# Two steps of a decode attention moved in TensorE's order: the turn of o with wo's matmuls, and the turn of q's second half

## The chip, the cores and the metric

The kernel runs on one core of one Trainium2 chip. Its time is the time on the device in microseconds of one execution. Before the change the median of 11 executions is 185.9 us (185.17 to 189.07).

Engines are named as in the profile: PE is TensorE (PEld its loading of weights), DVE VectorE, ACT ScalarE, POOL GpSimd, and SP SyncE, which issues the transfers.

## The reference

Two layers, each an attention with cached keys and values and a gated MLP, for one new token of each of four sequences. Both layers use the same weights and caches.

```python
# B=4, Sq=1, D=512, Hq=32, Hkv=8, Sk=8192, Dh=128, F=1792, W=2048, all bf16
def A(x):                                   # attention
    q = (x @ wq) as (B, 32, 1, 128)
    k, v = the last W=2048 positions of the caches, each kv head for 4 heads of q
    p = softmax(q k^T / sqrt(128))
    return (p v) as (B, 1, 4096) @ wo
def M(x):                                   # gated MLP
    return (sigmoid(x @ w_gate) * (x @ w_up)) @ w_down
x = x + A(layernorm(x)); x = x + M(layernorm(x))
x = x + A(layernorm(x)); x = x + M(layernorm(x))
```

## The kernel before

The whole program is a list of operations. Each `P.op` names an engine, what it reads and writes, the PSUM banks that it uses, and a function that emits the instructions. An operation depends on the last writers of what it reads, on the readers of what it writes, and, for a bank, on all operations of another engine that used the bank before. `_schedule` then puts the operations of each engine in an order by estimated durations, and `_assign_sync` turns the dependencies into semaphore waits. Each engine works through its own order. From the second layer's q on, `P.chain` is set: every TensorE operation then depends on the one written before it, so that TensorE's order is the order in which the program is written.

The transfers go to slots of one large tile in SBUF, `arena`. A slot is taken from a pool and given back when its last reader has been written down (`done`), so SP's order of issues follows from the order of the readers. The keys are loaded once and kept for both layers; all but a few tiles of V are loaded twice.

The second attention (`attn_second`) runs over eight units u = 0 to 7, one for each KV head h = 7 - u, all four sequences together. The first seven (`NW`) go through the wide path:

- `qx(u)`, in `q_unit`: four matmuls (L721) spread a head's q over a block layout, and ScalarE copies it to SBUF (L726).
- `score(u)`, in `softmax_unit`: four matmuls of a mask (L751) and 16 of K (L758) into one PSUM bank.
- `soft(u)`: the maximum on VectorE (L767, L771, L775, L779), the exponential on ScalarE (L782), which also gives the row sums.
- `turn(u)`, in `turn_p`: a permutation matmul (L795, called pp below), a copy on ScalarE (L797) and a 32 by 32 transpose on VectorE (L802). P is kept in one buffer, `prow`: the exponential of u+1 can start only when L802 of u has read it.
- `sum_up(u)`, in `sums`: POOL multiplies the row sums with a mask (L898), TensorE adds over partitions (L903), VectorE takes the reciprocal (L905), POOL spreads it (L908). The sum goes to bank `CB` for unit 0 and to bank `WB` for the others.
- `pv_wide(u)`: 16 matmuls of P with V (L925), VectorE's transpose of the bank (L933), the diagonal (L938), a move between partitions (L940), then on POOL an addition (L942) and the product with the reciprocals (L945).
- `o_back(u)`: two small matmuls (L959, called tr) that turn o to rows of wo in bank `WB` (bank `CB` for unit 6), and a copy on ScalarE (L965). It is written down as a function in `late` and called from the loop.
- `wo(u)`, in `wo_wide`: four matmuls with wo (L978).

The last unit takes another path (`pv_unit`, L844, L862, L1024), with the turn of unit 6 between its two V tiles. Then follow the second MLP's matmuls (L1170), and w_down's (L1210) in three pieces, each with a transfer of its own, and the output.

The second layer's q is made in two halves: the first (units 0 to 3) in `q_second`, the second (units 4 to 7) at the beginning of `attn_second`; `q_turn` transposes such a half on VectorE (L687) and scales it (L691).

The loop of the units in the kernel before:

```python
            for u in range(NW):
                if u == NW - 1:
                    wo(u - 1)
                op[u] = pv_wide(tag(u), hs[u], u % 2, v_tiles[(2, hs[u])])
                turn(u + 1)
                score(u + 2)
                soft(u + 2)
                ...
                sum_up(u + 1)
                qx(u + 3)
                if 0 < u < NW - 1:
                    wo(u - 1)
                if u < NW - 1:
                    op[u] = late.pop(("tr", tag(u)))()
```

Of the kernel before, what the change touches and what calls it, by code (L numbers as in the profile page):

```python
# [278 lines left out]
def build(nc, A_x, A_k, A_v, A_wq, A_wo, B_wg, B_wu, B_wd, out, cfg=None):  # L279
# [8 lines left out]
    NW = cfg.get("NW", 7)  # L288
# [33 lines left out]
    with es:  # L322
# [47 lines left out]
        P = _Plan()  # L370
# [4 lines left out]
        OBS = (4, 5)  # L375
# [13 lines left out]
        def c_dve(n, rate=None):  # L389
            return tm["dve_fix"] + n * (tm["dve_f32"] if rate is None else rate)  # L390
# [36 lines left out]
        def need(name):  # L427
            while name not in where:
                take_load()
            return where[name]  # L430
# [53 lines left out]
        def wq_part(k, c, i):  # L484

            if k == 0:
                return ("wq", c, k), i * SLOT
            return ("wq", (i, c // 2), k), (c % 2) * SLOT
# [33 lines left out]
        def load_v(h, bp, k, n_use):  # L522
# [7 lines left out]
             r=[("ones_f",)], w=[("e", 0)])  # L530
# [6 lines left out]
        for jh in range(2):  # L537
            for bp in range(2):
                for i in range(2):
# [7 lines left out]
                         r=[("ones_f",), ("perm",)], w=[("perm", jh, bp, i)])  # L547
# [5 lines left out]
             r=[("ones_f",)], w=[("msk_s",)])  # L553
        P.op("vector", "msk_s2", 100.0, lambda v: v.tensor_scalar(msk_s[:, :], msk_s[:, :], -1.0e30, None, ALU.mult),
             r=[("msk_s",)], w=[("msk_s",)])
        P.op("gpsimd", "msk_m", 200.0,
             lambda g: g.affine_select(msk_m[:, :], ones_f[:, 0:2], [[-1, 2]], ALU.is_equal, 0.0, base=0, channel_multiplier=1),
             r=[("ones_f",)], w=[("msk_m",)])
        P.op("vector", "sel_f", 200.0,
             lambda v: v.tensor_reduce(sel_f[:, :], perm[:, :].rearrange("p (g x) -> p x g", x=NR), AXX, ALU.add),  # L560
             r=perms, w=[("sel_f",)])
        P.op("gpsimd", "sel_b", 200.0, lambda g: g.tensor_copy(sel_b[:, :], sel_f[:, :]),
             r=[("sel_f",)], w=[("sel_b",)])
        P.op("vector", "sel_r", 100.0,
             lambda v: v.tensor_reduce(sel_r[:, :], sel_f[:, :].rearrange("p (g y) -> p y g", g=2), AXX, ALU.add),
             r=[("sel_f",)], w=[("sel_r",)])
        P.op("vector", "eyew", 200.0,
             lambda v: v.tensor_reduce(eyew[:, 96:128], ident.rearrange("p (a j) -> p j a", a=4), AXX, ALU.max),
             r=[("e", 0), ("eyew0",)], w=[("eyew",)])
        P.op("vector", "maskp", 200.0,  # L570
             lambda v: v.tensor_reduce(maskp[:, :], ident.rearrange("p (a j) -> p a j", a=4), AXX, ALU.max),
             r=[("e", 0)], w=[("maskp",)])
        P.op("vector", "maskb", 100.0,
             lambda v: v.tensor_reduce(maskb[:, :], maskp[:, :].rearrange("p (j b) -> p b j", j=2), AXX, ALU.max),
             r=[("maskp",)], w=[("maskb",)])
# [3 lines left out]
             r=[("eyew",)], w=[("maske",)])  # L579
        P.op("vector", "mod4", 100.0,  # L580
             lambda v: v.tensor_reduce(mod4[:, :], ey.rearrange("p (e m) -> p m e", m=REP), AXX, ALU.max),
             r=[("eyew",)], w=[("mod4",)])
# [4 lines left out]
             r=[("mod4",), ("maskp",)], w=[("selm",)])  # L587
# [4 lines left out]
             r=[("e", 0)], w=[("permo",)])  # L592
# [4 lines left out]
             r=[("sel_r",)], w=[("maskr",)])  # L597

        o = P.op("scalar", "x_in", 1300.0, lambda e: e.dma_start(x_nat, x_d), w=[("prow",)])
# [80 lines left out]
                if not (keep_last and c == NC - 1):  # L680
                    done(name)

        def q_turn(k, i, qb, buf=None, toks=(("e", 0), ("e", 1))):
            buf = ebuf[:, :] if buf is None else buf
            toks = list(toks)
            P.op("vector", "qt%d_%d" % (k, i), c_dve(512),
                 lambda v: v.transpose(buf, ps[:, qb, :].rearrange("p (x k t) -> p x t k", k=32, t=2)),  # L687
                 r=[("qrow", i)], w=toks, banks=(qb,))
            qi = qh[:, i * 64:(i + 1) * 64]
            return P.op("vector", "qc%d_%d" % (k, i), c_dve(64),  # L690
                        lambda v: v.tensor_tensor(  # L691
                            qi.rearrange("p (c b r) -> p c b r", c=4, b=NB),
                            buf.rearrange("p (r c y) -> p c y r", c=4, y=32)[:, :, 0:NB],
                            lnr[:, 0:NB].unsqueeze(1).unsqueeze(3).broadcast_to([128, 4, NB, REP]), ALU.mult),
                        r=toks + [("lnr", 0)], w=[("qh", i)])
# [42 lines left out]
        late = {}  # L738
# [135 lines left out]
        rest = {}  # L874
# [38 lines left out]
        def pv_wide(tag, h, k2, tiles):  # L913
            ob = OBS[k2]
            ew = ebuf[:, k2 * 256:(k2 + 1) * 256].bitcast(BF16).rearrange("p (g n x t) -> p g n t x", g=4, n=2, t=2)
            ss = dict((bp, need(name)) for bp, name in tiles)

            def e_pv(pe):
                last = None
                for n in range(4):  # L920
                    mq, t = n // 2, n % 2
                    for g in range(4):
                        jh, bp = g // 2, g % 2
                        src = tile_ap(ss[bp])[:, (jh * 16 + 8 * mq) * 128:(jh * 16 + 8 * mq + 8) * 128]
                        last = pe.matmul(ps[32 * g:32 * g + 32, ob, :], ew[:, g, mq, t],  # L925
                                         src.rearrange("p (m t d) -> p t m d", t=2, d=128)[:, t], start=(n == 0), stop=(n == 3))
                return last
            P.op("tensor", "PV" + tag, 16 * tm["pe_row"], e_pv,
                 r=tok(ss[0]) + tok(ss[1]) + [("e", k2)], w=[("pso", k2, 0), ("pso", k2, 1)], banks=(ob,))
            for bp, name in tiles:  # L930
                done(name)
            tv, o32, osh, rm, av = (rest[n, k2] for n in ("tv", "o32", "osh", "rm", "A"))
            P.op("vector", "tv" + tag, c_dve(512), lambda v: v.transpose(tv, ps[:, ob, :]),  # L933
                 r=[("pso", k2, 0), ("pso", k2, 1)], w=[("tv", k2)], banks=(ob,), after=(rest["op"],))

            def e_rd(v):
                dg = rest["dg", k2].rearrange("p (m y) -> p m y", m=4)[:, :, 0:128].rearrange("p m (q z) -> p q z m", z=32)[:, :, 0:8, :]
                return v.tensor_reduce(o32.rearrange("p (q x) -> p q x", x=8), dg, AXX, ALU.add)  # L938
            P.op("vector", "rd" + tag, c_dve(128), e_rd, r=[("tv", k2)], w=[("o32", k2)])
            P.op("vector", "sh" + tag, tm["dve_small"], lambda v: v.tensor_copy(osh[0:64, :], o32[64:128, :]),  # L940
                 r=[("o32", k2)], w=[("osh", k2)])
            P.op("gpsimd", "ad" + tag, 250.0, lambda v: v.tensor_tensor(o32[0:64, :], o32[0:64, :], osh[0:64, :], ALU.add),  # L942
                 r=[("o32", k2), ("osh", k2)], w=[("o32", k2)])
            P.op("gpsimd", "av" + tag, 500.0,
                 lambda v: v.tensor_tensor(  # L945
                     av[0:64, :].rearrange("p (x q e) -> p x q e", x=8, q=4),
                     o32[0:64, :].rearrange("p (q x) -> p x q", x=8).unsqueeze(3).broadcast_to([64, 8, 4, 8]),
                     rm[0:64, :].rearrange("p (x e) -> p x e", e=8).unsqueeze(2).broadcast_to([64, 8, 4, 8]), ALU.mult),
                 r=[("o32", k2), ("rm", k2)], w=[("av", k2)])
            late["tr", tag] = lambda: o_back(tag, k2, av)  # L950
# [101 lines left out]
        def attn_second():  # L1052
            hs = list(range(HKV))[::-1]

            def tag(u):
                return "2.%d" % u

            def turn(u):
                turn_p(2, tag(u), u % 2, PBS[0], u < NW)

            def qx(u):
                if u < HKV:
                    q_unit(tag(u), hs[u], u % 2)

            def score(u):
                if u >= HKV:
                    return
                softmax_unit(tag(u), hs[u], True, False)
                for bp in range(2):
                    pool.release(4 * hs[u] + 2 * bp)  # L1070
                fill()

            def soft(u):
                if u < HKV:
                    late.pop(tag(u))()

            def sum_up(u):
                if u < NW:
                    sums(tag(u), u % 2)
                elif u < HKV:  # L1080
                    sums_old(tag(u), u % 2)

            qx(0)
            q_mms(1, 0, OBS[1], (0, 1))
            qx(1)
            score(0)
            score(1)
            qx(2)
            soft(0)
            turn(0)  # L1090
            s = need(wq_part(1, NC - 1, 0)[0])
            left[wq_part(1, NC - 1, 0)[0]] += 1
            q_mms(1, 0, OBS[1], (2, 3))
            wide_buffers(s, P.ops[-1])
            sum_up(0)
            q_turn(1, 0, OBS[1], rest["tv", 1], [("tv", 1)])
            soft(1)
            op = {}

            def wo(u):  # L1100
                wo_wide(tag(u), hs[u], op[u], u % 2, u == 0, u == NW - 2)

            for u in range(NW):
                if u == NW - 1:
                    wo(u - 1)
                op[u] = pv_wide(tag(u), hs[u], u % 2, v_tiles[(2, hs[u])])
                turn(u + 1)
                score(u + 2)
                soft(u + 2)
                if u == NW - 1:  # L1110
                    wo_back()
                sum_up(u + 1)
                qx(u + 3)
                if 0 < u < NW - 1:
                    wo(u - 1)
                if u < NW - 1:
                    op[u] = late.pop(("tr", tag(u)))()
            u = NW

            def between():  # L1120
                wo_compact(tag(u - 1), hs[u - 1], late.pop(("tr", tag(u - 1)))(), (u - 1) % 2)
            wo_unit(tag(u), hs[u], pv_unit(tag(u), hs[u], u % 2, v_tiles[(2, hs[u])], between), u % 2, False, True)
# [143 lines left out]
        v_tiles = {}  # L1266
# [93 lines left out]
```

## Time and profile before

| | us |
|---|---|
| median of 11 runs | 185.9 |
| their range | 185.17 to 189.07 |
| profiled execution, its own time | 189.55 |
| span of that execution, first to last instruction | 187.8 |
| PE busy | 103.7 (55%) |
| DVE busy | 102.2 (54%) |
| ACT busy | 32.9 (18%) |
| POOL busy | 21.4 (11%) |
| transfers on SP's queue | 71.84 MB, 93.8% of the 16 DMA engines' span |
| L733, VectorE's transposes of K (first layer only) | 37.0, 32 of 1202 ns |
| L758, scores | 26.3, 256 of 548 ns |
| L925, P times V of the second attention | 9.6, 112 of 465 ns |
| L959 for DVE's L905, waited | 7.7 in 6 waits |

Matmuls that follow each other overlap, so a mean of 548 ns is not the time that one of them adds. Times of single pieces, such as 153.46, are microseconds from the start of the span. The profile's second part cuts the span in 40 slices of 4.7 us; each digit is a share in tenths. The chain that ended last is followed back from the last instruction, at each step to what released it.

### The profile page before, as it was taken

Reading aid. Unit: us, or ns where it says so; the run is one execution under the profiler, and the core shown is the slowest. Engines: PE = TensorE matmul, PEld = TensorE weight load, DVE = VectorE, ACT = ScalarE, POOL = GpSimd, SP = SyncE. Lnnn points to the kernel's source line nnn. Section 1 sums busy time; section 2 is a strip of 40 time slices with the busy share of each in tenths; the row PEclk is TensorE's granted clock in tenths of the full one; section 3 lists DMA queues with packets and bytes.
Section 4 is the critical chain, followed back from the end, with each engine's and each line's share of the span. In section 5 each row is a group of like instructions: output and inputs, shape, how many; then the busy total and the mean of one; then the engine's idle time right before and its main releaser. Section 6 shows DMA issues by size and latency. Waiting matters only on the chain.

```text
span 187.8 us, 3838 instructions
## 1 busy us (share of the span) xinstructions
PE 103.7 (55%) x1628; PEld 55.3 (29%) x1639; DVE 102.2 (54%) x253; ACT 32.9 (18%) x87; POOL 21.4 (11%) x86
## 2 busy tenths in 40 slices
PE   1434434754707436064367474358596767759692
PEld 1012121342403315033157422213222333326531
DVE  5209997467683554935645441226744666664243
ACT  2002032030212103011020010001323333332011
POOL 6000011010100101001010000000131333333000
PEclk9999999999999999999999999999955999995558
DMA  5999999999999999999999999999999999999700
GB/s 193 420 434 424 422 415 417 417 422 415 415 424 426 420 420 411 421 422 413 417 420 413 401 414 408 331 349 427 375 415 429 424 420 417 415 404 419 290 3 4
DMA packets 12305, 72.09 MB, mean 384 GB/s; under 512 B 1144, under 2 KB 1152, under 8 KB 5632
## 3 DMA queue, kind: packets, MB, share of 16 engines
q1 hardware_dynamic: 12280, 71.84, 93.8%
q8 instruction: 13, 0.21, 0.5%
q10 hardware_dynamic: 8, 0.00, 0.0%
q14 instruction: 4, 0.03, 0.0%
HBM read 71.83 MB, written 0.00 MB: 382 GB/s over the span
## 4 chain that ended last, share of the span: by engine, by line
PE 33%; DMA 27%; DVE 27%; issue 4%; SPq 4%; ACT 3%; DVEq 0%; ACTq 0%
DMA arena<-in_A_v_cache_dram 19%; DVE arena L733 11%; PE ps L758 9%; DMA arena<-in_A_wq_dram 6%; PE ps L844 5%; PE ps L925 5%; SPq L398 4%; DVE nmax L767 3%; DMA arena<-in_B_w_down_dram 3%; PE ps L751 3%; PE ps L1170 2%; DVE ebuf L802 2%; PE ps L1024 2%; DVE nmax L771 2%; ACT prow L782 2%
## 5 line engine op out<-in xcount | busy, mean ns | idle before, releaser
L733 DVE STREAM_TRANSPOSE arena<-arena 128x1024 f32<-128x1024 f32 x32 | 37.0, 1202 | 0.0
L758 PE MATMUL ps<-arena,qbd 128*32 128x512 bf16 x256 | 26.3, 548 | 0.0
L844 PE MATMUL ps<-ebuf,arena 128*128 128x8 bf16 x576 | 17.8, 168 | 9.0 <-DMA arena<-in_A_v_cache_dram 5.4
L751 PE MATMUL ps<-msk_m,msk_s 128*32 128x512 bf16 x64 | 9.0, 555 | 23.0 <-DVE arena L733 21.9
L767 DVE TENSOR_REDUCE nmax<-ps 128x1 f32<-128x512 f32 x16 | 10.9, 681 | 17.4 <-PE ps L758 17.2
L844 PEld LDWEIGHTS ps<-ebuf,arena 128*128 128x128 bf16 x576 | 16.8, 104 | 11.0 <-DMA arena<-in_A_v_cache_dram 6.5
L782 ACT ACTIVATE prow<-ps,nmax 128x512 bf16<-128x512 f32 x16 | 11.0, 688 | 35.2 <-DVE nmax L779 31.6
L726 ACT CAST qbd<-ps 128x256 bf16<-128x256 f32 x16 | 6.0, 372 | 51.7 <-PE ps L758 34.9
L674 PE MATMUL ps<-arena,xn 128*4 128x512 bf16 x64 | 7.9, 578 | 10.3 <-DMA arena<-in_A_wq_dram 7.9
L758 PEld LDWEIGHTS ps<-arena,qbd 128*32 128x32 bf16 x256 | 8.8, 126 | 11.0 <-issue 9.3
L797 ACT CAST prow<-ps 128x512 bf16<-128x512 f32 x16 | 9.4, 586 | 15.3 <-PE ps L795 5.3
L933 DVE STREAM_TRANSPOSE arena<-ps 128x512 f32<-128x512 f32 x7 | 5.0, 717 | 12.2 <-PE ps L925 12.2
L811 POOL CAST s<-psm 128x1 bf16<-128x1 f32 x9 | 1.7, 188 | 84.7 <-ACT prow L782 84.2
L925 PE MATMUL ps<-arena,ebuf 128*32 128x512 bf16 x112 | 9.6, 465 | 0.1
L751 PEld LDWEIGHTS ps<-msk_m,msk_s 128*32 128x32 bf16 x64 | 1.8, 102 | 24.8 <-DVE arena L733 19.0
L687 DVE STREAM_TRANSPOSE ebuf<-ps 128x512 f32<-128x512 f32 x3 | 2.2, 717 | 12.7 <-PE ps L674 12.6
L1170 PE MATMUL ps<-arena,xn 128*4 128x448 bf16 x64 | 7.0, 564 | 2.4 <-DMA arena<-in_B_w_up_dram 1.7
L655 ACT ACTIVATE lnv<-ps 128x4 f32<-128x4 f32 x4 | 0.7, 174 | 42.5 <-PE ps L651 42.5
L802 DVE STREAM_TRANSPOSE ebuf<-prow 128x256 f32<-128x256 f32 x16 | 7.0, 436 | 2.1 <-ACT prow L797 1.9
L721 PE MATMUL ps<-qh,eyew 32*128 32x64 bf16 x64 | 5.7, 220 | 4.1 <-ACT qbd L726 2.4
L852 DVE TENSOR_TENSOR onb<-ps,rinv 128x16 bf16<-128x16 f32 x9 | 1.7, 185 | 10.7 <-PE ps L844 10.7
L1024 PE MATMUL ps<-onp,arena 128*128 128x16 bf16 x144 | 5.3, 175 | 2.4 <-DVE onp L867 2.4
(105 smaller groups left out, 125.4 us busy)
## 6 DMA issues: line engine op xcount, KB each, us to landing
arena<-in_A_v_cache_dram SPq DMA_DIRECT2D x30, 1024.0 KB, 16.3
arena<-in_A_k_cache_dram SPq DMA_DIRECT2D x16, 1024.0 KB, 25.2
arena<-in_A_wq_dram SPq DMA_DIRECT2D x8, 1024.0 KB, 9.6
arena<-in_A_wo_dram SPq DMA_DIRECT2D x4, 1024.0 KB, 24.7
arena<-in_B_w_gate_dram SPq DMA_DIRECT2D x4, 896.0 KB, 14.1
arena<-in_B_w_up_dram SPq DMA_DIRECT2D x4, 896.0 KB, 15.9
arena<-in_B_w_down_dram SPq DMA_DIRECT2D x2, 1024.0 KB, 12.9
arena<-in_B_w_down_dram SPq DMA_DIRECT2D x1, 768.0 KB, 7.4
```

Of the source, the lines that this page charges most:

```text
L674: last = pe.matmul(ps[32 * hh:32 * hh + NB, qb, :], xn[:, c * NB:(c + 1) * NB], tile_ap(s)[:, o + hh * 512:o + (hh + 1) * 512], start=(c = ...
L733: P.op("vector", "T%d_%d" % (h, t), c_dve(1024), lambda v, v32=v32: v.transpose(v32, v32), r=[("slot", 4 * h + t)], w=[("slot", 4 * h + t)])
L751: last = pe.matmul(ps[32 * gi:32 * gi + 32, bank, :], msk_s[:, :], msk_m[:, :].unsqueeze(1).broadcast_to([128, 256, 2]), start=True, stop= ...
L758: last = pe.matmul(ps[32 * gi:32 * gi + 32, bank, :], qbd[:, q0:q0 + 32], kt[:, cp // 2, cp % 2, jh * NJ:(jh + 1) * NJ, :], start=False, s ...
L767: lambda v: v.tensor_reduce(nmax[:, k2:k2 + 1], ps[:, bank, :], AXX, ALU.max),
L782: lambda a: a.activation(prow[:, :].rearrange("p (m x t) -> p m x t", x=32, t=2), ps[:, bank, :].rearrange("p (m t x) -> p m x t", x=32, t ...
L797: P.op("scalar", "pc" + tag, c_act(512), lambda a: a.copy(prow[:, :], ps[:, pb, :]), r=[("ppb", pb)], w=[("prow",)], banks=(pb,))
L802: P.op("vector", "pt" + tag, c_dve(256), lambda v: v.transpose(et, prow[:, :].bitcast(F32)), r=[("prow",)], w=[("e", k2)])
L844: last = pe.matmul(ps[:, ob, bp * 8:bp * 8 + 8], src[:, j * 128:(j + 1) * 128], ev[:, j % 2, j % 16 // 2, x0:x0 + 8], start=(j == 0), stop ...
L925: last = pe.matmul(ps[32 * g:32 * g + 32, ob, :], ew[:, g, mq, t], src.rearrange("p (m t d) -> p t m d", t=2, d=128)[:, t], start=(n == 0) ...
L1024: last = pe.matmul(ps[:, WB, c * NR:(c + 1) * NR], tile_ap(s)[:, o + r_ * D + c * 128:o + r_ * D + (c + 1) * 128], ov[:, r_ * NR:(r_ + 1) ...
L1170: last = pe.matmul(ps[32 * g:32 * g + NB, OBS[n], 0:NF], xn[:, c * NB:(c + 1) * NB], tile_ap(s)[:, o:o + NF], start=(c == 0), stop=(c == N ...
```

## The change

Two things are moved; no instruction is added or taken away.

In the loop, `o_back` of a unit (L959 on TensorE, L965 on ScalarE) is no longer called at the end of that unit's turn of the loop. It is called in the next turn, behind P times V of the next unit and the permutation of the P after it. In TensorE's order `tr` of unit u-1 then stands behind L925 of u and L795 of u+1 and ahead of the scores of u+2. The matmuls with wo of unit u-1 stand at the end of turn u, as before. For the last wide unit the turn of unit 5 is called directly ahead of its wo, where it stood before too.

In the prologue, qx(2) is written behind the exponential and the permutation of unit 0, and the transpose of q's second half is given a dependency on unit 0's L802, so that on VectorE it stands behind it.

On ScalarE the copy L965 then stands behind L797, no longer ahead of it, and the copy L726 of qx(2) stands behind the first L782 and L797. On VectorE L802 of unit 0 and L687 change places. The orders of POOL and SP are the same as before.

```diff
-        def q_turn(k, i, qb, buf=None, toks=(("e", 0), ("e", 1))):
+        def q_turn(k, i, qb, buf=None, toks=(("e", 0), ("e", 1)), after=()):
...
-                 r=[("qrow", i)], w=toks, banks=(qb,))
+                 r=[("qrow", i)], w=toks, banks=(qb,), after=after)
...
             score(0)
             score(1)
-            qx(2)
             soft(0)
             turn(0)
+            qx(2)
...
-            q_turn(1, 0, OBS[1], rest["tv", 1], [("tv", 1)])
+            q_turn(1, 0, OBS[1], rest["tv", 1], [("tv", 1)], [o for o in P.ops if o.name == "pt2.0"])
...
+            def back(u):
+                op[u] = late.pop(("tr", tag(u)))()
+
             for u in range(NW):
                 if u == NW - 1:
+                    back(u - 1)
                     wo(u - 1)
-                op[u] = pv_wide(tag(u), hs[u], u % 2, v_tiles[(2, hs[u])])
+                pv_wide(tag(u), hs[u], u % 2, v_tiles[(2, hs[u])])
                 turn(u + 1)
+                if 0 < u < NW - 1:
+                    back(u - 1)
                 score(u + 2)
                 soft(u + 2)
...
                 if 0 < u < NW - 1:
                     wo(u - 1)
-                if u < NW - 1:
-                    op[u] = late.pop(("tr", tag(u)))()
             u = NW
```

## The prediction

> **What bounds the kernel now.** I read the chain that ended last first. Up to 127.3 us it goes through the transfers; from the third quarter of wq (landing at 127.3) to the end it holds no transfer at all. So the second attention and the second MLP, some 60 us, are bound by engines. Below, u is a unit (one KV head) of the second attention. The chain within one unit at full clock, TensorE's and VectorE's pieces:
>
> ```profile
> 153.10 0.09 DVE arena L905
> 153.33 0.19 PE ps L959 x2
> 153.52 1.01 PE ps L925 x16
> 154.55 0.73 DVE arena L933
> 155.30 0.45 DVE arena L938
> 155.99 0.45 DVE ebuf L802
> 156.43 0.59 DVE nmax L767
> 157.69 0.21 DVE nmax L779
> 157.90 0.09 DVE arena L905
> 158.13 0.19 PE ps L959 x2
> 158.32 0.32 PE ps L925
> ```
>
> It is a closed loop of 4.80 us (153.52 to 158.32): P times V (L925), VectorE's transpose of it, the diagonal, the transpose of P (L802), the whole maximum of the next scores (L767 to L779), the reciprocal (L905), then the turn `tr` (L959), and only then the next P times V. The wait behind it:
>
> ```profile
> PE ps L959 <- DVE arena L905: 7.7, 6, 1.5
> ```
>
> `tr` of unit u writes bank WB, from which VectorE's reciprocal of unit u+1 reads, and that stands last in VectorE's order. P times V of u+1, whose own operand L802 wrote 1.8 us earlier, stands behind `tr`.
>
> Then the clock, by the stretches, whose columns are time, PE, PEld, DVE, ACT, POOL busy, granted clock, DMA share, GB/s:
>
> ```profile
> 136.00:140.70 4.70, 4.68 (x38) 1.22 (x39) 2.01 (x6) 1.36 (x3) 1.51 (x4) 0.50 1.01 418
> 140.70:145.50 4.80, 3.10 (x34) 1.32 (x37) 2.35 (x8) 1.54 (x5) 0.60 (x2) 0.50 1.01 423
> 155.10:159.90 4.80, 3.51 (x57) 1.49 (x49) 3.20 (x11) 1.80 (x6) 1.51 (x4) 1.00 1.01 415
> ```
>
> The first two units ran at half clock: P times V starts at 136.02, 142.70, 148.66, then every 4.80. That is 148.66 - 136.02 - 2 x 4.80 = 3.04 us more than at full clock. (The 9s before 131 are not borne out: L758's 16 matmuls take 1.71 to 1.74 us there, as at half clock.) Last, the transfers:
>
> ```profile
> DMA  5999999999999999999999999999999999999700
> GB/s 193 420 434 424 422 415 417 417 422 415 415 424 426 420 420 411 421 422 413 417 420 413 401 414 408 331 349 427 375 415 429 424 420 417 415 404 419 290 3 4
> ```
> ```profile
> arena<-in_B_w_down_dram SPq DMA_DIRECT2D x1, 256.0 KB, 15.9
> ```
>
> The last piece of w_down (256 KB) is issued at 163.5 and lands 15.9 us later, at 179.4, though its matmuls (L1210, 184.18 to 185.13) come at some 185.0. The engines are thus 5.6 us behind the last transfer in this execution; the stream has been full since its start and does not get shorter by this change.
>
> **What the Trainium skill says.** "TensorE: Matmul & The Clock Gate", in "What overlaps and what doesn't", has matmuls start and end strictly in program order; the trace agrees: L925 waits behind L959. The same page, "What's actually happening", says the array runs at half clock until it has been busy for a window of about 3.4 us and falls back after an idle one; here the scores' 20 matmuls take 2.32 us (138.38 to 140.70) at 0.50 and 1.34 (154.76 to 156.10) at 1.00. "DMA: Bandwidth & Descriptors", "Specifications", gives a fabric ceiling of 435 GB/s; the slices above show 415 to 430, so the stream has no reserve.
>
> **Part 1, the turn behind P times V.** No instruction is added or removed. TensorE's order of a unit was PV(u), pp(u+1), scores(u+2), sum, qx, WO(u-1), tr(u); it becomes PV(u), pp(u+1), tr(u-1), scores(u+2), sum, qx, WO(u-1). On ScalarE the copy behind `tr` moves behind the copy of P (L797). PV(u+1) now waits only for its P and its V.
> What closes the loop next: pp(u+1) needs the exponential of u+1, which needs its maximum, which needs its scores, which stand behind pp(u) in TensorE's order. Its sum at full clock: L767 to L779 1.55 (156.35 to 157.90), to the exponential 0.04 (157.94), from there to pp 0.83 (133.11 to 133.94), pp to scores 0.32 (154.44 to 154.76), two matmuls of `tr` now between them 0.13 (153.33 to 153.46), scores 1.34, to the maximum 0.06 (140.70 to 140.76): 4.27 us. That it isn't less is checked on the engines. VectorE's own list, L933 to L905, is 3.44 (154.55 to 157.99). TensorE needs 0.32 + 0.13 + 2.09 (scores to WO's end, 154.76 to 156.85) + 1.05 = 3.59; PV(u) then ends about as the reciprocal does and VectorE goes on without a gap. The added `tr` in front of the scores waits for POOL's product (L945), which ends 0.67 + 0.25 + 0.2 us after L940, about 2.8 us ahead of its new place, so at nothing; without that cover it would go into the loop one to one. ScalarE's moved copy of 0.17 delays only the copy of qx (L726), needed a unit later. POOL's and SP's lists stay as they are, and SP waits for scores and P times V, which come earlier. The unit falls by 4.80 - 4.27 = 0.53; between pp(2) and pp(6) there are four such.
>
> **Part 2, the prologue.** qx(2) moves behind pp(0). Its copy (L726, 132.84 + 0.37) stood before the first exponential on ScalarE: that starts at 132.53, after L779's end at 132.49, not at 133.11, 0.58 earlier. pp(0) 133.36; qx(2) 0.28 and the last eight matmuls of q's second half follow and end at 134.55 instead of 134.86. POOL's mask and product (0.24 + 0.32, with their gaps 0.63) and the sum give sum(0) at 135.23 and PV(0) at 135.57, against 136.02. The second half of q's turn (L687, 0.72) falls behind the first L802, which then ends at 134.87 instead of 135.96; so the second exponential starts at 134.91, not 136.00. q's second half is wanted only for unit 4, some 10 us later: nothing. Then pp(1) 136.62, the scores end at 138.28, L802 at 138.50, the maximum runs 138.45 to 140.00, pp(2) stands at 140.87. Four units of 4.27: pp(6) at 157.95, the last maximum at 159.80, in the profiled execution 166.16, and at full clock 166.16 - 3.04 - 0.22 (PV at 163.04 took 1.27, not 1.05) = 162.90. So 3.1 us less at equal clock, 6.4 less than this execution. From there on (tr(5), WO(5), PV(6), the tail) the order is unchanged.
>
> **The sum.** Engines: 187.8 - 6.4 = 181.4 us of span. Transfers: 179.4, the last eight matmuls of L1210 0.2, then from L1210's end to the span's end 2.7 (185.13 to 187.83): 182.3. The transfers end last. On the way the V tiles nearly hold: a tile of 1024 KB takes 2.49 us at 421 GB/s, so counted back from 179.4 over the MLP's 5.25 MB (13.1 us) and the tiles of units 6 and 7 (10.0) V of unit 5 is whole at 156.3, wanted at 156.2; V of unit 6 at 161.3, wanted at 162.7. Outside the span the profiled execution has 189.55 - 187.8 = 1.75, so 182.3 + 1.75 = 184.05. This execution is 3.65 above the median of 185.9; at full clock mid-kernel it would be 187.8 - 3.26 + 1.75 = 186.3, near that median, so I take the transfers' end over as it stands: 184.0 us, 1.0% less.
>
> **Rivals.**
> A: the stream ends earlier in other executions. The slices of 331, 349 and 375 GB/s cost, against 418, 0.98 + 0.78 + 0.48 = 2.2 us. Without them the floor is 181.8 and the engines set the end: 185.9 - 3.1 = 182.8, less up to 0.6 for an earlier wq. For it: the same loads of V ran at 415 and more a little later. Against: two of the three slices hold wq's loads, in another shape than V's. 182.2 to 183.4.
> B: half the gain only, for a part of the loop stays at half clock, or a wait that the trace of before doesn't show (bounds: nothing and 0.53 a unit, the whole gain) enters: 184.6 to 185.5. For it: the execution shows two half-clock stretches. Against: TensorE is busier, 3.59 of 4.27 where it was 3.5 of 4.80.
> C, slower: TensorE stays at half clock. There a unit costs on TensorE alone pp 0.53, tr 0.15, scores 2.32, sum 0.31, qx 0.43, WO 0.7, PV 1.90: 6.3 us, 2.1 above 4.27. The engines are 0.9 under the transfers' end; to pass 186.3 takes 3.1 us more, that is 1.5 units, about 9.5 us, at half clock in most executions, as long as the stretch in the page (136 to 145.5). Beyond that it is slower, to 189 with three or four units. Against: such units leave TensorE no idle time, and just such a dense stretch (128.2 to 132) came before the clock's rise.
> D: no change, since the turn's wait comes back in front of the scores (its partner POOL late): the 2.8 us of cover speak against it. 185.6 to 186.2.
>
> **How the numbers follow.** Transfers' end 184.0 (183.5 to 184.6): 0.49. A 0.25, B 0.14, C 0.08, D 0.04. About 0.2% (0.4 us) is what a measurement here can tell from no change. Faster 0.49 + 0.25 + 0.14 = 0.88, same 0.04, slower 0.08. The range takes in A and B: 182.2 to 185.5.
>
> **What would show it.** Right: L925 of neighbouring units 4.2 to 4.4 us apart instead of 4.80; L959 no longer waiting for L905; L925 waiting for WO in its own queue or L802; the chain ending in a transfer of w_down and L1210 broken up by it; the first exponential near 132.5. Wrong: an interval over 4.6 at full clock (a loop I missed), clock digits of 5 between 136 and 165, or an end of the stream away from 179.4. The weakest step is taking one execution's stream for all.

## The result and the profile after

| | before | after |
|---|---|---|
| median, us | 187.44 (47 runs, 185.11 to 190.34) | 184.16 (12 runs, 183.53 to 185.55) |
| profiled execution, its time / span | 189.55 / 187.8 | 184.09 / 182.4 |
| P times V of neighbouring units apart at full clock, from the third unit on | 4.80 | 4.28 to 4.29 |
| first exponential starts | 133.11 | 132.52 |
| last maximum starts | 166.16 | 159.63 |
| last piece of w_down lands | 179.4 | 179.2 |

The ratio is 0.988, 95% interval 0.985 to 0.991: faster by 1.2%. It is formed from the undisturbed executions alone, so it lies nearer to one than the quotient of the two medians. The median before is over more executions than the 185.9 of the first part, and 1.5 us higher; why that matters comes below.

The page of the changed kernel: granted clock, the transfers' share and rate in 40 slices of the span (here 4.56 us each), and the chain that ended last by engine.

```profile
PEclk9999999999999999999999999999999999995555
DMA  5999999999999999999999999999999999999970
GB/s 197 428 428 420 424 420 419 415 422 420 416 420 420 420 420 412 420 426 420 407 425 419 406 403 409 353 344 420 411 395 419 429 412 424 424 411 405 413 294 20
...
DMA 42%; DVE 26%; PE 19%; ACT 4%; SPq 4%; issue 3%; POOL 0%; DVEq 0%; ACTq 0%
...
arena<-in_B_w_down_dram SPq DMA_DIRECT2D x1, 256.0 KB, 15.8
```

Three things are to be seen. The stretch at half clock in the first units is gone in this execution. The stream has the same dip (353 and 344 GB/s) at the same place as before, and the last piece of w_down takes 15.8 us where it took 15.9. And transfers now have the largest share of the chain that ended last, which says that the end has changed hands. The chain itself, in the middle of a unit and at its end (start, duration, what):

```profile
151.07 0.70 DVE nmax L767
...
152.70 0.79 ACT prow L782 x2
...
153.53 0.39 PE ps L795
153.92 0.13 PE ps L959 x2
154.05 0.33 PE ps L751 x4
154.38 0.95 PE ps L758 x16
155.36 0.70 DVE nmax L767
...
162.52 16.09 DMA arena<-in_B_w_down_dram
178.66 0.60 PE ps L1214 x16
179.29 0.41 PE ps L1214 x8
```

From one maximum to the next (151.07 to 155.36) it is 4.29 us, through the exponential, the permutation L795, the two matmuls of the turn, and the scores. P times V is no longer in it. And from 162.52 on only transfers of w_down count: the piece of 512 KB, issued there, lands at 178.61 and lets its 16 matmuls start, and the last piece, of 256 KB, lands at 179.2, ahead of its 8. The whole second MLP runs beside these transfers. The timeline of TensorE, changed kernel, at w_down's matmuls (L1214, which was L1210; start, duration, then in brackets the idle time before and what ended it):

```profile
177.40 1.02 PE L1214 MATMUL ps<-arena,hT 128*4 128x128 bf16 x32 [1.16 <-DMA arena<-in_B_w_down_dram]
178.66 1.02 PE L1214 MATMUL ps<-arena,hT 128*4 128x128 bf16 x24 [0.23 <-DMA arena<-in_B_w_down_dram]
```

The 56 matmuls come in two lots, the second behind a transfer.

**A wait that isn't one.** The list of waits of the changed kernel has these lines (waiter, releaser: us in all, times, longest):

```profile
PEld ps L795 <- ACT prow L782: 16.2, 12, 1.8
...
PE ps L959 <- DVE arena L938: 3.9, 3, 1.5
```

Read alone, the second says that the turn now waits for VectorE's diagonal. The timeline says otherwise:

```profile
144.96 0.39 PE L795 MATMUL ps<-prow,perm 128*128 128x512 bf16 x1 [0.88 <-ACT prow L782]
145.28 0.20 PE L959 MATMUL ps<-msks,arena 64*128 64x8 bf16 x2
...
149.57 0.20 PE L959 MATMUL ps<-msks,arena 64*128 64x8 bf16 x2 [1.21 <-DVE arena L938]
```

In the unit at 145 the matmul of L795 is recorded, and L959 follows it with no idle time. In the unit at 149.57 the matmul of L795 is missing from the trace (its weight load stands at 149.24, after 1.37 us of waiting for L782), so the idle time is put down to the next instruction on the list and to whatever ended shortly before it. POOL's product, which the turn really needs, had ended at 146.55 (L945, 145.87 + 0.68), 3.0 us before 149.57.

### The profile page after: what moved, and what is told of

Its sections match the earlier page's. It is cut to its first block, busy times and chain, and to the rows that moved or that the text cites. A ratio compares the mean times of both kernels' runs of the same rounds, so it can differ in the third digit from the quotient of the medians.

```text
span 182.4 us, 3840 instructions
## 1 busy us (share of the span) xinstructions
PE 100.1 (55%) x1627; PEld 54.8 (30%) x1639; DVE 102.0 (56%) x253; ACT 32.9 (18%) x87; POOL 21.3 (12%) x86
## 4 chain that ended last, share of the span: by engine, by line
DMA 42%; DVE 26%; PE 19%; ACT 4%; SPq 4%; issue 3%; POOL 0%; DVEq 0%; ACTq 0%
DMA arena<-in_A_v_cache_dram 23%; DMA arena<-in_B_w_down_dram 9%; DVE arena L733 9%; PE ps L758 7%; DMA arena<-in_A_wq_dram 6%; DMA arena<-in_B_w_up_dram 5%; DVE nmax L767 5%; SPq L398 4%; ACT prow L782 3%; PE ps L751 3%; DVE nmax L771 2%; DVE mxt L775 2%; PE ps L844 2%; DVE arena L933 1%; PE ps L1024 1%
## 5 line engine op out<-in xcount | busy, mean ns | idle before, releaser
L782 ACT ACTIVATE prow<-ps,nmax 128x512 bf16<-128x512 f32 x16 | 11.0, 687 | 37.7 <-DVE nmax L779 35.0
L726 ACT CAST qbd<-ps 128x256 bf16<-128x256 f32 x16 | 6.0, 372 | 46.2 <-PE ps L758 34.9
L674 PE MATMUL ps<-arena,xn 128*4 128x512 bf16 x64 | 7.9, 578 | 8.9 <-DMA arena<-in_A_wq_dram 7.8
L797 ACT CAST prow<-ps 128x512 bf16<-128x512 f32 x16 | 9.4, 586 | 11.0 <-PE ps L795 2.8
L802 DVE STREAM_TRANSPOSE ebuf<-prow 128x256 f32<-128x256 f32 x16 | 7.0, 436 | 4.7 <-ACT prow L797 4.6
L687 DVE STREAM_TRANSPOSE ebuf<-ps 128x512 f32<-128x512 f32 x3 | 2.2, 717 | 13.2 <-PE ps L674 13.1
L925 PE MATMUL ps<-arena,ebuf 128*32 128x512 bf16 x112 | 7.3, 380 | 0.0
L795 PEld LDWEIGHTS ps<-prow,perm 128*128 128x128 bf16 x16 | 1.6, 100 | 17.0 <-ACT prow L782 16.2
```

The lines of the kernel that those rows point to most:

```text
L674: last = pe.matmul(ps[32 * hh:32 * hh + NB, qb, :], xn[:, c * NB:(c + 1) * NB], tile_ap(s)[:, o + hh * 512:o + (hh + 1) * 512], start=(c = ...
L782: lambda a: a.activation(prow[:, :].rearrange("p (m x t) -> p m x t", x=32, t=2), ps[:, bank, :].rearrange("p (m t x) -> p m x t", x=32, t ...
L797: P.op("scalar", "pc" + tag, c_act(512), lambda a: a.copy(prow[:, :], ps[:, pb, :]), r=[("ppb", pb)], w=[("prow",)], banks=(pb,))
L802: P.op("vector", "pt" + tag, c_dve(256), lambda v: v.transpose(et, prow[:, :].bitcast(F32)), r=[("prow",)], w=[("e", k2)])
```

## The experiments

**1. The loop alone.** The changed kernel with the prologue as it was.

```diff
             score(1)
+            qx(2)
             soft(0)
             turn(0)
-            qx(2)
...
-            q_turn(1, 0, OBS[1], rest["tv", 1], [("tv", 1)], [o for o in P.ops if o.name == "pt2.0"])
+            q_turn(1, 0, OBS[1], rest["tv", 1], [("tv", 1)])
```

> The moved turn alone; qx(2) and the transpose of q's second half stand as before. Theory (the transfers' end sets the time, the prologue's 0.45 us lie in the slack before it): units still 4.29 us apart, everything after the first P times V 0.4 to 0.5 us later than with both parts, the last piece of w_down lands at 179.2 and the time is that of both parts, 184.2 within 0.3 us. Rival (the prologue's gain reaches the end): 184.6 to 185.0. Second rival (the prologue keeps the clock up): a half-clock stretch from 136 on, and 185 or more.

Measured: 183.78 us (183.47 to 184.4, 4 runs) beside 187.74 (35 runs) of the kernel before on that chip; ratio 0.984 (0.978 to 0.990). That is the time of both parts, 184.16, or a little under it. P times V of unit 0 was expected 0.4 to 0.5 us later than with both parts; in the profiled execution it came 1.1 us earlier (134.27 for 135.37), since all from wq on came earlier by as much (the first eight matmuls of q's second half, L674, at 126.12 for 127.18). The end of its chain:

```profile
161.93 16.09 DMA arena<-in_B_w_down_dram
...
178.06 0.60 PE ps L1214 x16
...
178.69 0.41 PE ps L1214 x8
```

The transfers end it as well; the last piece lands at 178.6 here. Whatever the prologue saves the engines has nowhere to show once the loop is faster.

**2. The prologue alone.** The changed kernel with the loop as it was.

```diff
-            def back(u):
-                op[u] = late.pop(("tr", tag(u)))()
-
             for u in range(NW):
                 if u == NW - 1:
-                    back(u - 1)
                     wo(u - 1)
-                pv_wide(tag(u), hs[u], u % 2, v_tiles[(2, hs[u])])
+                op[u] = pv_wide(tag(u), hs[u], u % 2, v_tiles[(2, hs[u])])
                 turn(u + 1)
-                if 0 < u < NW - 1:
-                    back(u - 1)
...
                     wo(u - 1)
+                if u < NW - 1:
+                    op[u] = late.pop(("tr", tag(u)))()
```

> The prologue alone; the turn of o stands at the end of its unit as before. Theory: the first exponential at 132.5, the first P times V 0.4 to 0.5 us earlier, units 4.80 apart at full clock, the end set by the engines: 0.3 to 0.6 us less than the kernel before at equal clock (ratio 0.997 to 0.999); if the denser prologue also keeps the clock up, the gain on the median is larger, up to 2 us. Rival (most of the gain lies here): under 185.0 us.

Measured: 186.6 us (184.77 to 187.48, 12 runs) beside 187.74; ratio 0.999 (0.995 to 1.003). The median is 1.1 us lower, but the interval holds one: a gain of up to 0.5% is not excluded, nor a small loss. None of the 12 executions passed 187.48, while the kernel before reached 190.73; whether the prologue helps to keep the clock up, which the expectation held possible, these runs do not settle. The turn in TensorE's timeline and the end of the chain, in two views:

```profile
145.39 0.19 PE L959 MATMUL ps<-msks,arena 64*128 64x8 bf16 x2 [1.28 <-DVE arena L905]
150.18 0.19 PE L959 MATMUL ps<-msks,arena 64*128 64x8 bf16 x2 [1.30 <-DVE arena L905]
```
```profile
181.40 1.69 PE ps L1210 x56
```

The old loop is there, 4.79 us with the wait for the reciprocal, and the engines end last: all 56 matmuls of w_down in one lot, with no transfer in front.

**3. The turn where it was, in another bank.** Is it the place of `tr` that costs, or the bank that it shares with the sums? The kernel before, in which `o_back` writes to bank CB, in columns that nothing else there uses.

```diff
         def o_back(tag, k2, av):
-            q0 = 16 + k2 * 16
-            tb = CB if tag == "2.%d" % (NW - 1) else WB
+            q0 = 288 + k2 * 16
+            tb = CB
```

> The order of before; only the bank of the turn of o changes: all units write it to the bank of qx, columns 288 and on, so that it no longer waits for the reciprocal of the next unit, but for the copy of qx. Theory (it was the wait for the reciprocal, not the place in the order as such): the turn starts when POOL's product is done, some 0.9 us earlier within a unit, P times V is off VectorE's loop, units 4.1 to 4.4 us apart at full clock, time 184.0 to 184.6. Rival (the place counts: the turn stands in front of P times V and POOL's product ends late): units 4.6 to 4.8 apart, 185.3 to 186.

Measured: 184.38 us (184.04 to 184.71, 4 runs), ratio 0.987 (0.981 to 0.992): as fast as the change, with the order of before. TensorE's timeline and the end of the chain:

```profile
148.65 0.19 PE L959 MATMUL ps<-msks,arena 64*128 64x8 bf16 x2 [0.24 <-ACT qbd L726]
148.78 1.05 PE L925 MATMUL ps<-arena,ebuf 128*32 128x512 bf16 x16
...
152.81 0.19 PE L959 MATMUL ps<-msks,arena 64*128 64x8 bf16 x2 [0.24 <-ACT qbd L726]
152.94 1.05 PE L925 MATMUL ps<-arena,ebuf 128*32 128x512 bf16 x16
```
```profile
163.38 15.77 DMA arena<-in_B_w_down_dram
...
179.20 0.59 PE ps L1210 x8
```

The turn still stands ahead of P times V, and no longer waits for the reciprocal. The unit takes 4.16 us, less than the 4.29 of the changed order, because the two matmuls of the turn (0.13) stand outside the loop through the scores. What cost 4.80 - 4.16 = 0.64 us a unit was the dependency through the bank, not the place of the turn as such; moving it away is one of two ways round it. The wait is one that the program puts in, by its rule that operations of different engines on one bank wait for each other; a kernel without that wait was not run. The end is the transfers' again, so the shorter unit brings nothing more.

**4. Does a busier TensorE keep the clock up?** The kernel before with 16 matmuls of a mask into a free bank behind qx(2).

```diff
             qx(2)
+
+            def e_fill(pe):
+                last = None
+                for n in range(16):
+                    gi = n % 4
+                    last = pe.matmul(ps[32 * gi:32 * gi + 32, SB[1], :], msk_s[:, :],
+                                     msk_m[:, :].unsqueeze(1).broadcast_to([128, 256, 2]), start=True, stop=True)
+                return last
+            P.op("tensor", "fill", 16 * tm["pe_row"], e_fill, r=[("msk_s",), ("msk_m",)], w=[("fill",)], banks=(SB[1],))
```

> The kernel before with 16 matmuls of the mask (about 1 us at full clock) put into TensorE's gap between the scores of unit 1 and the first permutation; nothing reads them. Theory (the spread of the kernel before from 185 to 190 us comes from TensorE's clock[...]): no half-clock stretch between 136 and 146, median 0.5 to 2 us below that of before, and a narrower spread. Rival (the spread comes from the transfers): the same median within 0.3 us and the same spread.

Measured: 186.69 us (184.6 to 188.26, 22 runs) beside 187.74 (35 runs), ratio 0.999 (0.995 to 1.002). The median is 1.05 us lower and the spread 3.7 us where it was 5.6, as the theory had it, but the interval holds one: inconclusive. Two stretches of its profiled execution (time, PE, PEld, DVE, ACT, POOL busy, granted clock, DMA share, GB/s):

```profile
136.00:140.70 4.70, 3.04 (x43) 1.24 (x43) 3.53 (x13) 1.78 (x5) 1.50 (x4) 1.00 1.02 425
...
146.80:150.30 3.50, 3.50 (x35) 1.26 (x31) 2.38 (x5) 0.63 (x2) 0.91 (x2) 0.51 1.01 421
```

The clock was full where the filler would have helped, and fell ten microseconds later instead. What makes it fall in one execution and not in another stays open.

**5 and 6. Take the last transfers away.** If the transfers set the end of the changed kernel and not of the one before, then leaving out the last two loads of w_down shortens the first and not the second. The same edit in both:

```diff
-                load(("wd", a, k), 1, "bw_8k", ((b - a) * D, wd_d[:, a:b, :], False))
+                if k < NG or a == 0:
+                    load(("wd", a, k), 3 if k >= NG else 1, "bw_8k", ((b - a) * D, wd_d[:, a:b, :], False))
...
-                    name = ("wd", a, k)
+                    name = ("wd", 0, k)
```

> The changed kernel without its last two transfers (the second layer's pieces of w_down of 512 and 256 KB); their matmuls read the first piece instead, so the product with w_down is computed from part of its rows only. All instructions of the engines stay. Theory (the last transfers set the end by some 1.2 us): the 56 matmuls with w_down run through without a break from about 177.4, and the time falls by 0.9 to 1.4 us against the changed kernel, to 182.7 to 183.3. Rival (the engines set the end): no change, 184.0 to 184.3.

> The kernel before without the same two transfers, the same part left out. Theory (there the engines come after the last transfer, by 1 us at the highest clock and by 5 us in the profiled execution): no change against the kernel before, and the fastest executions at 185.1 to 185.4 as there. Rival (the stream as a whole holds the kernel back): 0.9 us less or more.

Measured: the changed kernel without them 183.3 us (182.92 to 184.15, 6 runs), 0.86 less than 184.16. The kernel before without them 187.0 (185.14 to 190.85, 22 runs) beside 187.46, ratio 0.997 (0.993 to 1.000). At the same high clock (0.967 and 0.968) it takes 185.14 to 186.4 without (7 executions) and 185.01 to 186.19 with them (9): nothing that can be told. The changed kernel as it is was not run beside experiments 5 to 8, so the 0.86 compares two series; in the same series the changed kernel with 0.7 us of work added (experiment 7) took 184.36, 1.06 more than without the loads. The chain of the changed kernel without the two loads:

```profile
157.50 19.17 DMA arena<-in_B_w_down_dram
...
176.71 1.69 PE ps L1215 x56
```

Even then a transfer stands in front, now of the piece that is still loaded. So the floor is the stream's, and the engines are close behind it.

**7 and 8. How close?** The changed kernel with VectorE's transpose in front of the last hT made twice, and five times; the extra ones write the same values again.

```diff
-                P.op("vector", "gt%s%d" % (nm, k), c_dve(NF), ...)
+                for _ in range(2 if n and last else 1):
+                    P.op("vector", "gt%s%d" % (nm, k), c_dve(NF), ...)
```

In run 8 the 2 is a 5.

> The changed kernel with the transpose before the product of the second MLP (ahead of the matmuls with w_down) done twice, 0.7 us more on the engines' path. Theory: the engines have 1.2 us of slack before the last transfer, so 0 to 0.1 us more, 184.1 to 184.3. Rival (engines set the end): 0.7 us more, 184.8.

> The same transpose five times, 2.8 us more on the engines' path. Theory: 2.8 less the slack of 1.2, 1.4 to 1.7 us more, 185.6 to 185.9. Rival (engines set the end): 2.8 us more, 186.9 to 187.

Measured: 0.7 us more work gives 184.36 (6 runs), 0.2 over the changed kernel, which is within the spread; 2.8 us more gives 185.91 (185.22 to 187.01, 22 runs), 1.75 over it. So 2.8 - 1.75 = 1.05 us of the five-fold work was hidden. TensorE at w_down, first the kernel with two, then the one with five:

```profile
177.41 0.82 PE L1215 MATMUL ps<-arena,hT 128*4 128x128 bf16 x32 [1.92 <-DMA arena<-in_B_w_down_dram]
```
```profile
180.04 1.66 PE L1215 MATMUL ps<-arena,hT 128*4 128x128 bf16 x56 [3.84 <-DVE hT L1202]
```

With two, the releaser is a transfer still; with five it is hT, and the 56 matmuls run in one lot. The slack of the engines in the changed kernel lies between 0.7 and 2.8 us, about 1.

**9. One transfer less.** If the stream is the floor, one tile of V (1024 KB, 2.5 us at 421 GB/s) kept from the first layer should lower it.

```diff
-    KEEP_V = cfg.get("KEEP_V", 2)
+    KEEP_V = cfg.get("KEEP_V", 3)
```

> The changed kernel with three tiles of V kept in SBUF from the first layer instead of two: one transfer of 1024 KB less, the result unchanged. Theory (the transfers' end sets the time, the engines come 1.0 to 1.2 us before it): the last piece lands about 2.5 us earlier, near 176.7, if the kept slot delays no other load; then the engines set the end, 182.8 to 183.4, 0.9 us less than the changed kernel. Rival (the slot that is kept is missed by the loads of the second layer's q): those loads land later, the engines start later and it is as slow as the changed kernel or slower, 184 to 186.

Measured: 187.63 us (186.54 to 189.09, 6 runs) beside 187.06 of before, ratio 1.011 (1.004 to 1.017). That is 3.5 us over the changed kernel's 184.16, and no faster than the kernel before; by how much slower than that one it is hangs on the clock (186.54 to 187.04 at 0.958 and 0.959, where the kernel before took 186.11 and 186.68). The last piece landed at 178.4 (162.7 + 15.7), only 0.8 us ahead of the 179.2 of the changed kernel. The stream lost what it had been spared: two of its 40 slices are at 296 and 298 GB/s, where the lowest of the changed kernel's own dip is 344. That the loads wait for slots to come free, and so don't simply move up, is the likely reason; it was not tested. And something else became late: VectorE's transposes that bring the kept data back (L517). First the changed kernel, then the one with three kept tiles, VectorE's timeline:

```profile
128.26 2.66 DVE L517 STREAM_TRANSPOSE arena<-ps 128x512 f32<-128x512 f32 x4 [1.52 <-PE ps L674]
130.84 0.68 DVE L767 TENSOR_REDUCE nmax<-ps 128x1 f32<-128x512 f32 x1
```
```profile
131.11 2.66 DVE L517 STREAM_TRANSPOSE arena<-ps 128x512 f32<-128x512 f32 x4 [4.09 <-PE ps L758]
133.70 0.65 DVE L767 TENSOR_REDUCE nmax<-ps 128x1 f32<-128x512 f32 x1
```

They start 2.85 us later and stand ahead of the first maximum, which moves by as much (130.84 to 133.70); P times V of unit 0 starts at 139.04 where it started at 135.37. The engines end last again.

**10 and 11. The same with the other way round the bank, and alone.** Run 10 is the kernel before with the third tile kept, the prologue of the change, and the turn in bank CB; run 11 is the kernel before with the third tile kept and nothing else (the edits are those of 9 and 3, and the lines of the prologue that experiment 1 takes back).

> The kernel before with three tiles of V kept, the prologue's part of the change, and instead of the moved turn the turn's result in the bank of qx. Theory: units 4.16 us apart, as measured for that bank, against 4.29 for the moved turn, over five units 0.5 to 0.6 us less for the engines, and no transfer in the way: 182.3 to 183.0. Rival (the transfers or the start of the second attention bind again): 183.0 or more, not below the changed kernel with three tiles kept.

> The kernel before with three tiles of V kept: the same transfer less. Theory (its engines come after the last transfer anyway): no change against the kernel before, the executions of the highest clock at 185.0 to 185.5. Rival (fewer bytes help by themselves): 1 us less or more.

Measured: 186.28 us (184.69 to 187.98, 14 runs), ratio 1.000 (0.996 to 1.003), and 191.5 (190.45 to 193.47, 6 runs), ratio 1.029 (1.022 to 1.036). In run 10 the unit is 4.14 to 4.17 us, and the late start of the attention (P times V of unit 0 at 139.24) gives back what that wins. Run 11 was expected to stand still and lost 2.9%: its first units also ran at half clock (P times V at 138.49, 145.17, 151.86, so 6.7 us apart). How much of it is the late start and how much the clock was not separated. No version measured beats the changed kernel by more than the spread; the loop alone (183.78) equals it.

## Why the prediction was right, point by point

184.0 us was predicted and 184.16 measured, in the range and in the likeliest case.

**The loop before.** That the turn waits for the reciprocal through bank WB, and holds P times V up behind it, is shown by experiment 3: the bank alone, with no change of order, takes the unit from 4.80 to 4.16 us.

**What closes the loop next.** Predicted 4.27 us through the scores, measured 4.29 through just these pieces. By the timeline from 144.95: permutation to turn 0.33, turn 0.13, scores to maximum 1.38, maximum 1.58 (1.55 was taken), then 0.04 and 0.83. The cover of the turn by POOL was 3.0 us where 2.8 was worked out.

**The prologue.** First exponential 132.52 (132.53 predicted), P times V of unit 0 135.37 (135.57), last maximum 159.63 (159.80), so 6.5 us ahead of the execution before, where 6.4 was worked out; at w_down's first matmul (177.40 for 184.18) it is 6.8. These are times of the profile, and the steps of the engines held to 0.2 us up to the last maximum. That the first exponential hit its mark is luck in part: its time moves with wq, and experiment 3, with the prologue of before, has it at 132.49. What the prologue wins shows in differences. From the first exponential to the second it is 2.35 to 2.40 us with it (changed kernel, experiments 2, 5, 7 and 8; 2.57 and 2.58 in 10 and 9, where the attention starts late) and 2.88 to 2.90 without it (kernel before, 1, 3, 4, 6 and 11). From the first eight matmuls of q's second half to P times V of unit 0 it is 8.16 to 8.20 us with it in those five; without it 8.74 to 8.89 in the kernel before, 3 and 6, but 8.15 in experiment 1. There the 16 scores of unit 1 took 1.11 us, at full clock, where they took 1.49 to 1.64 in those three, so that the copy of qx(2) was over when the maximum was. ScalarE's timeline in experiment 1 (its L779 ends at 131.33):

```profile
131.00 0.37 ACT L726 CAST qbd<-ps 128x256 bf16<-128x256 f32 x1 [3.12 <-PE ps L721]
131.37 0.69 ACT L782 ACTIVATE prow<-ps,nmax 128x512 bf16<-128x512 f32 x1
```

So 0.04 us were to be won there, not 0.58: the prologue takes away a wait that depends on the clock. In the time of the kernel it is worth nothing that could be measured beside the loop (experiment 1), and at most 0.5% alone (experiment 2). The prediction had counted it among the 3.1 us of the engines at equal clock, about 1.0 of them (3.1 - 4 x 0.53), and not said that it hangs on the clock, nor that behind the transfers' floor it falls away first.

**The transfers' end.** Predicted 182.3 of span, measured 182.4. Experiments 5 to 8 show it from both sides: without the last loads the changed kernel gains 0.86 us and the one before nothing; work added to the engines is hidden up to about 1.05 us, where the sum had them 0.9 under the transfers. Taking one execution's stream for all was called the weakest step. It held: in the eight profiled executions whose loads are all there the last piece landed between 178.6 and 179.8. The reading of the slices, "415 to 430", was a little narrow: between the ramp at the start and the end of the stream, and outside the dip, its own line goes from 401 to 434 GB/s.

**What the change is worth.** This step was off: "at full clock mid-kernel it would be 187.8 - 3.26 + 1.75 = 186.3, near that median". The kernel before has no one time. Among its 35 executions on the chip of the first four experiments the five with a mean clock of 0.967 or 0.968 took 185.12 to 185.38, 1 us less than 186.3; those at 0.946 or below took 186.6 and more. The changed kernel took 184.09, 184.4 and 184.67 at 0.946 to 0.948 and 183.96, 184.05 and 185.55 at 0.968 to 0.970: no such slope, though from three on each side. The mean clock also does not say where the half-clock stretches lie: in the changed kernel's profile (0.948) they come from 163.4 on, where the transfers hide them, in the one before (0.933) from 136 to 145.5 as well. So the gain is some 1.2 us at a high clock (185.2 to 184.0) and some 3 at a lower one (187.39 at 0.945 to 184.4 at 0.947), and the predicted 1.9 us (185.9 to 184.0) happened to lie between. Of the 3.1 us that the engines win at equal clock, about 1 shows at the high clock, and about 1 became the slack of experiment 8. The rest, some 0.9, would fit the prologue's share, which was nothing at full clock (above); no profile of the kernel before at a high clock was taken, so this stays an estimate. The prediction's number was right because the end that it named depends on the clock only where the engines lose more than that slack; the size of the gain hangs on a median of 11 executions that 47 moved by 1.5 us.

**The rivals.** A, an earlier end of the stream, didn't come: the slices of 353, 344 and 395 GB/s are there as before. B, half the gain: no new wait entered (the one that the list of waits offers is a missing record), though the time at a high clock before makes the gain about as small as B's. C, half clock in the first units: the clock was full from 132.7 to 163.4 in the profiled execution, and no execution passed 185.55. D, the turn's wait coming back in front of the scores: it has 3.0 us of cover.

That matmuls keep program order, as the Trainium skill has it ("TensorE: Matmul & The Clock Gate", "What overlaps and what doesn't") is borne out twice: P times V waited for a turn that it did not need, and was freed both by moving that turn and by freeing the turn itself.

## What to carry to other kernels

Before moving an instruction that others queue behind, ask what it waits for: here a PSUM bank shared with a small sum made the wait, and two changed lines of addresses did as much as a new order. Work out two ends separately, the engines' and the transfers', and take the later; then measure how far the other is behind, by adding work until the time moves, because what any further saving on the engines can bring stops at the first. And take a kernel's time at its own clock: where engines set the end it moves with the clock, where transfers do it doesn't as long as the engines' slack (about 1 us here) lasts, so a change that hands the end over gains most in the executions whose clock was low.

## What was not expected of the hardware

Being busy alone did not decide the clock. In the changed kernel it is full at 3.50 to 3.62 us of TensorE's work in 4.7 to 4.8:

```profile
136.00:140.70 4.70, 3.50 (x51) 1.32 (x44) 3.96 (x12) 1.73 (x4) 1.61 (x5) 1.00 1.01 415
140.70:145.50 4.80, 3.62 (x55) 1.72 (x60) 3.56 (x12) 1.93 (x6) 1.82 (x5) 1.00 1.00 422
```

In the kernel with the filler it was at half in a stretch in which TensorE hardly stopped (3.50 of 3.50 in experiment 4), and just before it, at full clock, TensorE had worked 3.48 us of 4.80 (140.7 to 145.5). The half-clock stretches lasted 3.4 us with the prologue alone (134.8 to 138.2) and in experiment 3 (134.9 to 138.3), and 3.5 in experiment 4, which fits the window of about 3.4 us that the Trainium skill gives ("TensorE: Matmul & The Clock Gate", "What's actually happening"). That the clock falls after an idle window, as the same section has it, is not what experiment 4 shows. What starts such a stretch was not found, so that the stretch is gone in the changed kernel's profiled execution is not claimed for the change. The end of the changed kernel runs at half clock too, from 163.4 on: w_down's 56 matmuls, which took 0.95 us at full clock before, take 1.69 in one lot at half (experiments 2 and 5), and in the changed kernel the transfers hide it.

Fewer bytes did not mean an earlier end: 1024 KB less, 2.5 us at the stream's rate, moved the last landing by 0.8 us (experiment 9) and delayed the engines by 2.85.
